# Four numerator tiles and six raw-row tiles in a linear attention followed by two feed-forward layers

## The chip, the cores and the metric

The kernel runs on one core of a Trainium2 chip. The metric is the time of one execution in microseconds (us) on the device, as the median of several runs. The engines are called TensorE (PE; its weight loads are PEld), VectorE (DVE), ScalarE (ACT), GpSimd (POOL) and SyncE (SP). Each runs its own instructions in the order in which they were written for it; an instruction that has to wait holds back all that stand behind it on its engine. GpSimd and SyncE issue most of the DMA transfers.

## What is computed

```
def _attn_ref(q, k, v, w_phi):            # q, k, v: 4 x 8 x 576 x 64
    def phi(x):
        proj = np.einsum('bhsd,df->bhsf', x, w_phi)              # f = 128
        proj = proj - np.max(np.abs(proj), axis=-1, keepdims=True)
        return np.concatenate([np.exp(proj), np.exp(-proj)], axis=-1)
    q_p, k_p = (phi(q), phi(k))
    kv = np.einsum('bhsf,bhsd->bhfd', k_p, v)
    z = np.sum(k_p, axis=2)
    num = np.einsum('bhsf,bhfd->bhsd', q_p, kv)
    den = np.einsum('bhsf,bhf->bhs', q_p, z)[..., None] + 1e-06
    return num / den

x = attention output as 2304 x 512
h = np.maximum(np.maximum(x @ w1, x @ w2), x @ w3)               # 768 wide
x = h @ w_out                                                    # 512 wide
h = x @ w_in                                                     # 2048 wide
g = np.maximum(h, 0.0) + alpha * np.minimum(h, 0.0)
out = g @ w_out2                                                 # 2304 x 512
```

## The kernel before

The kernel works through attention and the layers of the two feed-forward blocks. The attention goes pair by pair: four batches with four pairs of heads each, sixteen pairs in the loop at lines 467 to 489. For each pair, `keys` builds the features of the keys and multiplies them with the values (line 306, tile `kvp`); `queries`, which runs one pair behind, builds the features of the queries and the numerators: `num` (line 346) multiplies them into one PSUM bank `pn` at a time, and ScalarE copies each bank to a tile `nd` (line 357). One head's `nd` holds the numerators in one half of the partitions and the denominator in the rows of the other, so a pair takes two `nd` tiles.

After that GpSimd gathers the denominators by DMA into `dc` (line 388), moves the second head's numerators into the first tile (line 389), and, once VectorE has formed the reciprocals (lines 390 and 391), writes them out to `r_d` (line 393) and reads them back spread over the partitions into two raw tiles `xr` (line 400). `make_x` then multiplies `xr` with `nd` (line 414, GpSimd in the first pairs, VectorE in the others) and splits the result into a high part `x` (line 64, ScalarE) and a low part (line 70), the operands of layer 1. A tile `nd` is free again only after the product of line 414, a raw tile `xr` only after the split.

Layer 1 (`layer1`, line 436) takes groups of twelve matmuls of 288 columns, `p`, 48 units of three groups; a unit of a batch needs the `x` of all four pairs of that batch. The units of one batch are written between the pairs of the next, and those of the last batch behind the last pair (line 639). From the end of the last keys on, the weights of the later layers are staged: SyncE loads them into three tiles `st` (line 509), ScalarE and VectorE convert them (lines 77, 80, 84 and 86), and part of them goes out to `q_d` again (line 543). The staging tiles lie in the memory that the pool with the keys' tiles leaves. Then come layer 2 (`p`, line 691), layer 3 (`sums`, `pb`, `pc`, line 789) and layer 4 (`acc`, line 877).

The order of the instructions on each engine is written by a scheduler, which goes by priorities (the `high_priority` blocks), by what is ready in its own model and by which tiles are free: an instruction that needs a tile is placed only where one of that tag is free. So the number of buffers of a tag changes the order of all engines. `nd` lies in the pool `lp`, `xr` in the pool `xs_`; the pools that open after them take over that memory.

Of the kernel before, what the change touches and what calls it, by code (L numbers as in the profile page):

```python
# [9 lines left out]
F32 = mybir.dt.float32  # L10
# [11 lines left out]
P = 128  # L22
B, H, S, D = 4, 8, 576, 64
# [8 lines left out]
CH = S // 2  # L32
# [15 lines left out]
def tile_kernel(ctx: ExitStack, tc: tile.TileContext, qT, kT, tails, v, w_phi, w1, w2, w3, w_out, w_in, w_out2, alpha, out):  # L48
# [20 lines left out]
    def sub(eng, dst, src, hi):  # L69
        eng.tensor_tensor(dst, src, hi.bitcast(F32), op=ALU.subtract)  # L70
# [38 lines left out]
    def bank(tag, bufs, nm):  # L109
        return ps.tile([P, 512], F32, tag=tag, bufs=bufs, name=nm)  # L110
# [3 lines left out]
    xs_ = l1_ctx.enter_context(tc.tile_pool(name="xs", bufs=1, side="left"))  # L114
# [4 lines left out]
    def at(shape, dtype, name, tag=None, bufs=1):  # L119
        pool = ap if (tag or name) in KEYS_ONLY else lp  # L120
        return pool.tile(shape, dtype, name=name, tag=tag or name, bufs=bufs)
# [37 lines left out]
    def plain_kv(pair):  # L159
        return pair[0] < 2  # L160
# [57 lines left out]
    def project_queries(pair):  # L218
        ops = features(pair, "q")
        for g, tiles in enumerate(GROUPS):  # L220
            pp = at([P, 4, P], F32, tag="pp", bufs=2, name="pp")
            less_max(*project(ops, tiles), pp)
            yield g, tiles, pp
# [39 lines left out]
    def products(dst, ops, **kw):  # L263
        for i, (x, y) in enumerate(ops):
            nc.tensor.matmul(dst, x, y, start=i == 0, stop=i == len(ops) - 1, **kw)  # L265
# [69 lines left out]
    def queries(pair):  # L335

        parts = ("q",) if plain_kv(pair) else ("qh", "ql")
        qf = []
        for n, (o, w) in enumerate(CHUNKS):
            qf.append([])  # L340
            for x in parts:
                tag = f"qh{n}" if x != "ql" and pair[1] % 2 * len(x) != 1 else f"ql{n}"
                qf[n].append(at([P, 2, 2, w], F32 if plain_kv(pair) else F32R, tag=tag, bufs=1, name=x))
        nd = [at([P, S], F32, tag="nd", bufs=3, name="nd") for _ in range(2)]

        def num(n):
            o, w = CHUNKS[n]
            kv = kvs_of[pair]
            for h in range(2):
                pn = bank("p1", 3, "pn") if pair[0] == 0 else bank("pn", 1, "pn")  # L350
                ops = []
                for s in range(2):
                    q_ = [t[:, h, s] for t in qf[n]]
                    k_ = [t[:, h, s] for t in kv]
                    ops += [(k_[0], x) for x in q_] + [(x, q_[0]) for x in k_[1:]]
                products(pn[:, :w], ops)
                A.activation(nd[h][:, o : o + w], pn[:, :w], AF.Copy)  # L357

        def tail():
            yield 2, (0,), tail_of[pair]  # L360

        for g, tiles, pp in chain(project_queries(pair), tail()):
            o, w = (0, 2 * P, SM)[g], ST if g == 2 else 2 * P
            pt = bank("pn" if pair[0] == 0 and g == 1 else "pt", 1, "pt")
            for i in range(len(tiles)):
                for h in range(2):
                    c = h * len(tiles) * P + i * P
                    nc.tensor.transpose(pt[:, c : c + P], pp[:, 2 * i + h], ident)  # L368
            n = min(g, 1)
            dst = [t[:, :, :, o - CHUNKS[n][0] : o - CHUNKS[n][0] + w] for t in qf[n]]  # L370
            if plain_kv(pair):
                e = dst[0]
            else:
                e = at([P, 2, 2, 256], F32, tag="qe", bufs=2, name="qe")[:, :, :, :w]
            pv = pt[:, : 256 * len(tiles)].rearrange("p (h s) -> p h s", h=2)[:, :, -w:]
            A.activation(e[:, :, 0], pv, AF.Exp)
            A.activation(e[:, :, 1], pv, AF.Exp, scale=-1.0)
            if not plain_kv(pair):
                (hi_dve if g == 1 else hi_act)(dst[0], e)
                sub(V, dst[1], e, dst[0])  # L380
            yield
            if g != 1:
                num(n)
        yield
        dc = at([P, S // D], F32, tag="dc", bufs=2, name="dc")
        for h in range(2):
            dr = D * (1 - h)
            nc.gpsimd.dma_start(dc[h * D : (h + 1) * D], nd[h][dr : dr + 1].rearrange("a (p n) -> a p n", p=D))
        nc.gpsimd.dma_start(nd[0][D:], nd[1][D:])
        V.tensor_scalar(dc, dc, EPS, None, op0=ALU.add)  # L390
        V.reciprocal(dc, dc)
        rows = r_d[pair[0], pair[1]]
        nc.gpsimd.dma_start(rows.rearrange("h (p n) -> (h p) n", p=D), dc)
        raw = []
        for c in range(2):
            xr = raw_tile()
            for h in range(2):
                r = slice(h * D, (h + 1) * D)
                src = rows[h : h + 1, c * CH : (c + 1) * CH]
                nc.gpsimd.dma_start(xr[r], src.to_broadcast([D, CH]))  # L400
            raw.append(xr)
        waiting.append((pair, nd[0], raw))
        if pair[0] == 0 or pair[1] == NPAIR - 1:
            make_x(False)
# [3 lines left out]
    def make_x(pinned=True):  # L408

        pair, num_, raw = waiting.pop(0)  # L410
        res = []
        for c, xr in enumerate(raw):
            e = G if i_of(pair) < NPAIR - 1 else V
            x = e.tensor_tensor(xr, num_[:, c * CH : (c + 1) * CH], xr, op=ALU.mult)
            if pinned:
                tc.keep_in_program_order(x)
            xh, xl = x_tiles(c)
            if e is G:
                G.tensor_copy(xh, xr)
            else:  # L420
                hi_act(xh, xr)
            sub(e, xl, xr, xh)
            res.append((xh, xl))
        xs[pair[0]].append(res)

    def raw_tile():
        return xs_.tile([P, CH], F32, tag="xr", bufs=3, name="xr")

    def x_tiles(half):
        t = x_tile(half)  # L430
# [36 lines left out]
    for i, pair in enumerate(pairs):  # L467
        if i + 1 < len(pairs):
            load_pair(pairs[i + 1])
        with tc.high_priority(offset=(0, SOON, NOW, NOW)[pair[0]]):  # L470
            if i == PLAIN - 1:
                hi_dve(wph, wraw)
                sub(V, wpl, wraw, wph)
            run(*([at_priority(LATER, queries(last))] if last else []), keys(pair))
            last = pair
        count = CONVERT_IN[i] if i < len(CONVERT_IN) else 0
        for j in range(count):
            for _ in range(min(count, 4) if j == 0 else int(j + 3 < count)):
                fetch(begun[pair])
            with tc.high_priority(offset=LAST if i < NPAIR - 1 else 0):  # L480
                n = sum(len(x) for x in w)
                run(split_w123(n // 3, n % 3))
        u0 = 3 * (i - NPAIR) - LAG
        for u in range(u0, u0 + 3):
            if u >= 0:
                c, f = (u % 2, u // 2) if u < 12 else (u // NF1 % 2, u % NF1)
                layer1(u // 12, c, f, xs[u // 12], w[f])
        if waiting:
            make_x()
    ap_ctx.close()  # L490
    sp = ctx.enter_context(tc.tile_pool(reuse_waits="tile", name="sp", bufs=1, side="right"))
    with tc.high_priority(offset=NOW):
        run(queries(last))
# [128 lines left out]
    def load_h(c, kk):  # L622
        hi, lo = x_tile(c % 2), x_tile(c % 2)
        for k in range(2) if c == 0 else (slice(None),):
            if c == 0:
                hr = raw_tile()
                nc.sync.dma_start(hr, h_d[2 * kk + k, :, :CH])
            else:
                hr = early.pop(0) if c == 1 else fetch_h(c, kk)
            hi_act(hi[:, k], hr)  # L630
            sub(V, lo[:, k], hr, hi[:, k])
        for k in range(2):
            hs[c, 2 * kk + k] = (hi[:, k], lo[:, k])
# [29 lines left out]
    def double(tag, nm):  # L663
        t = ps.tile([P, 2, 512], F32, tag=tag, bufs=2 if tag == "da" else 1, name=nm)
        return t, t[:, :, :CH]
# [153 lines left out]
    for n, (tp, q) in enumerate(units):  # L819
# [4 lines left out]
        _, pb = double("db", "pb")  # L824
# [4 lines left out]
        _, pc = double("dc", "pc")  # L829
# [128 lines left out]
```

## Time and profile before

| | us |
|---|---|
| time, median of 3 runs | 883.45 (882.95 to 883.57) |
| the profiled execution | 883.95 |
| its span in the profile | 882.2 |
| TensorE busy in it | 868.6 (98%) |
| VectorE, ScalarE, GpSimd busy | 644.8, 506.8, 142.8 |

Busy time of TensorE is counted from pipelined matmuls whose ends are modelled, so neighbours overlap; how fast it works is read from the distance between starts. A time in a timeline or a chain is counted from the start of the span. The bracket behind a row says how long the engine was idle before it and what ended that. In the names `a<-b`, `a` is the tile written and `b` what is read.

### The profile page before, as it was taken

Reading aid. Unit: us, or ns where it says so; the run is one execution under the profiler, and the core shown is the slowest. Engines: PE = TensorE matmul, PEld = TensorE weight load, DVE = VectorE, ACT = ScalarE, POOL = GpSimd, SP = SyncE. Lnnn points to the kernel's source line nnn. Section 1 sums busy time; section 2 is a strip of 40 time slices with the busy share of each in tenths; the row PEclk is TensorE's granted clock in tenths of the full one; section 3 lists DMA queues with packets and bytes.
Section 4 is the critical chain, followed back from the end, with each engine's and each line's share of the span. In section 5 each row is a group of like instructions: output and inputs, shape, how many; then the busy total and the mean of one; then the engine's idle time right before and its main releaser. Section 6 shows DMA issues by size and latency. Waiting matters only on the chain.

```text
span 882.2 us, 17448 instructions
## 1 busy us (share of the span) xinstructions
PE 868.6 (98%) x6631; PEld 856.1 (97%) x6631; DVE 644.8 (73%) x1214; ACT 506.8 (57%) x1037; POOL 142.8 (16%) x250
## 2 busy tenths in 40 slices
PE   9999999999999999969999999999999999999998
PEld 8888999999999999969999999999999999999998
DVE  5578999778677767859964354746478999988781
ACT  4566676757764765666853354646477663544440
POOL 0354212213122222311101101111111000000000
PEclk9999999999999999989999999999999999999999
DMA  6445652313222149986556663655347756543321
GB/s 233 144 152 169 205 166 75 90 53 91 84 77 76 36 141 355 361 284 227 160 175 196 223 206 130 205 190 184 117 155 249 275 161 196 147 135 120 120 73 48
DMA packets 72227, 142.98 MB, mean 162 GB/s; under 512 B 9152, under 2 KB 36176, under 8 KB 72144
## 3 DMA queue, kind: packets, MB, share of 16 engines
q1 hardware_dynamic: 57696, 100.29, 35.9%
q0 software_dynamic: 12576, 37.92, 12.7%
q10 hardware_dynamic: 1872, 3.67, 1.3%
q8 instruction: 52, 0.85, 0.4%
q14 instruction: 31, 0.25, 0.1%
HBM read 93.07 MB, written 46.34 MB: 158 GB/s over the span
## 4 chain that ended last, share of the span: by engine, by line
PE 89%; DMA 5%; DVE 3%; ACT 1%; issue 1%; POOL 0%; ACTq 0%; DVEq 0%; POOLq 0%
PE p L265 22%; PE acc L877 20%; PE sums L789 12%; PE p L691 9%; PE pc L789 6%; PE pj L265 5%; PE pn L265 5%; PE kvp L306 3%; PE pb L789 3%; PE kvp L293 3%; DMA st<-in_w_out 2%; PE pt L368 2%; DMA st<-in_w_in 1%; DMA dc<-nd 1%; DMA nd<-nd 0%
## 5 line engine op out<-in xcount | busy, mean ns | idle before, releaser
L265 PE MATMUL p<-x,w123t 128*128 128x288 f32 x1728 | 253.2, 299 | 6.9 <-ACT x L64 6.9
L265 PEld LDWEIGHTS p<-x,w123t 128*128 128x128 f32 x1728 | 236.4, 190 | 8.2 <-ACT x L64 7.2
L789 PE MATMUL sums<-x,wi 128*128 128x288 f32 x768 | 107.6, 295 | 0.0
L877 PE MATMUL acc<-wq,o 128*128 128x256 f32 x864 | 105.5, 283 | 0.0
L877 PEld LDWEIGHTS acc<-wq,o 128*128 128x128 f32 x864 | 104.2, 189 | 0.0
L789 PEld LDWEIGHTS sums<-x,wi 128*128 128x128 f32 x768 | 103.9, 188 | 0.0
L877 PE MATMUL acc<-wq,x 128*128 128x256 f32 x648 | 78.1, 280 | 0.0
L877 PEld LDWEIGHTS acc<-wq,x 128*128 128x128 f32 x648 | 77.0, 188 | 0.0
L691 PE MATMUL p<-x,wo 128*128 128x288 f32 x576 | 76.6, 295 | 0.0
L691 PEld LDWEIGHTS p<-x,wo 128*128 128x128 f32 x576 | 76.5, 188 | 0.0
L808 DVE SCALAR_TENSOR_TENSOR g<-neg,al,g 128x576 f32<-128x576 f32 x64 | 50.3, 812 | 23.6 <-ACT neg L807 23.6
L212 DVE TENSOR_REDUCE mx<-pj 128x4 f32<-128x512 f32 (+1 forms) x80 | 50.3, 630 | 17.2 <-PE pj L265 17.0
L797 ACT ACTIVATE s<-sums 128x576 f32<-128x576 f32 x48 | 31.0, 647 | 42.0 <-PE sums L789 41.9
L455 POOL DMA_DIRECT2D h_d<-ho x48 | 28.9, 602 | 147.4 <-DVE ho L453 133.6
L809 POOL DMA_DIRECT2D g_d<-g x32 | 22.9, 715 | 166.1 <-DVE g L808 149.3
L357 ACT ACTIVATE nd<-pn 128x256 f32<-128x256 f32 (+1 forms) x64 | 26.4, 419 | 39.6 <-PE pn L265 25.2
L77 ACT ACTIVATE wt<-st 128x512 f16<-128x512 bf16 x38 | 30.1, 796 | 27.3 <-DMA st<-in_w_out 16.9
L293 PEld LDWEIGHTS kvp<-v,ke 128*128 128x128 f32 x320 | 40.9, 191 | 3.0 <-ACT ke L246 0.5
L807 ACT ACTIVATE neg<-g 128x576 f32<-128x576 f32 x64 | 40.1, 675 | 6.2 <-DVE g L839 5.9
L293 PE MATMUL kvp<-v,ke 128*128 128x128 f32 x320 | 42.6, 277 | 0.1
L64 ACT ACTIVATE o<-wt 128x512 fp32r<-128x512 f32 x45 | 27.4, 626 | 24.9 <-PE acc L877 15.1
L245 ACT ACTIVATE ke<-pj,mx 128x128 f32<-128x128 f32 x96 | 36.7, 382 | 7.5 <-DVE mx L212 7.5
(160 smaller groups left out, 1765.0 us busy)
## 6 DMA issues: line engine op xcount, KB each, us to landing
g_d<-g POOLq DMA_DIRECT2D x32, 576.0 KB, 3.6
a<-g_d SPq DMA_DIRECT2D x36, 512.0 KB, 4.6
st<-in_w_out SPq DMA_DIRECT2D x22, 512.0 KB, 6.1
wst<-in_w SPq DMA_DIRECT2D x18, 512.0 KB, 4.4
st<-in_w_in SPq DMA_DIRECT2D x16, 512.0 KB, 4.6
yr<-y_d SPq DMA_DIRECT2D x28, 288.0 KB, 3.5
v<-in_v SPq DMA_DIRECT2D x16, 480.0 KB, 4.2
q_d<-wt SPq DMA_DIRECT2D x28, 256.0 KB, 6.6
```

The lines of the kernel that those rows point to most:

```text
L77: order(A.activation(half[:, :, 1].bitcast(F16), lanes[:, :, 3].bitcast(BF16), AF.Copy))
L212: V.tensor_reduce(mx, pv, axis=AX.X, op=ALU.max, apply_absolute_value=True, negate=True)
L245: A.activation(ev[:, a, 0], pv[:, a], AF.Exp, bias=mx[:, a : a + 1])
L265: nc.tensor.matmul(dst, x, y, start=i == 0, stop=i == len(ops) - 1, **kw)
L293: nc.tensor.matmul(kvp[:, j * P : (j + 1) * P], e[:, c], rv[:, t, j // 2 : j // 2 + 2].rearrange("p a d -> p (a d)"), start=first, stop=t ...
L455: nc.gpsimd.dma_start(h_d[f, :, o : o + CH], ho)
L691: nc.tensor.matmul(p2[m // 2][1][:, m % 2], x, y, start=k + n == 0, stop=k == NF1 - 1 and n == 2)
L789: nc.tensor.matmul(dst[:, j], a, b, start=start and n == 0, stop=n == len(ops) - 1, skip_group_check=True)
L797: A.activation(s, src, AF.Copy)
L807: A.activation(neg, gv[:, j], AF.Relu, scale=-1.0)
L808: V.scalar_tensor_tensor(gv[:, j], neg, al[:, f + j : f + j + 1], gv[:, j], op0=ALU.mult, op1=ALU.add)
L877: nc.tensor.matmul(acc[i], x, y, start=half == 0 and f == 0 and n == 0 and place[i][1] == 0, stop=half == 1 and f == 3 and n == 2, skip_gr ...
```

## The change

The tag `nd` gets four buffers instead of three, and the tag `xr` six instead of three. No instruction is added or taken away; the scheduler writes another order. The two pools grow by 2304 and 3456 bytes in each partition.

```
--- before.py
+++ after.py
@@ -341,7 +341,7 @@
-        nd = [at([P, S], F32, tag="nd", bufs=3, name="nd") for _ in range(2)]
+        nd = [at([P, S], F32, tag="nd", bufs=4, name="nd") for _ in range(2)]
@@ -424,7 +424,7 @@
     def raw_tile():
-        return xs_.tile([P, CH], F32, tag="xr", bufs=3, name="xr")
+        return xs_.tile([P, CH], F32, tag="xr", bufs=6, name="xr")
```

In the rows of the order that follow, tiles carry the numbers in which the code makes them: `p1_` is a group of layer 1, `pn_4885`, `pn_4922` and `pn_4930` are numerators of the last pair, `nd_4850` and `nd_4851` its two tiles, `x_4952` its first `x`, and `st_` and `wt_` are weight loads and what they are converted to. TensorE around the last numerator of the last pair, before:

```order
L265 MATMUL p1_4789<-x_3588,w123t_1364 128x288 x3
L265 MATMUL p1_4802<-x_2621,w123t_1372 128x288 x3
L265 MATMUL p1_4802<-x_2992,w123t_1372 128x288
L265 MATMUL pn_4930<-qh_4848,kvh_4695 128x320
L265 MATMUL pn_4930<-ql_4849,kvh_4695 128x320
L265 MATMUL pn_4930<-qh_4848,kvl_4696 128x320
```

The same place after the change:

```order
L265 MATMUL p1_4407<-x_3359,w123t_1756 128x288 x3
L265 MATMUL p1_4407<-x_3584,w123t_1756 128x288 x3
L265 MATMUL pn_4930<-qh_4848,kvh_4695 128x320
L265 MATMUL pn_4930<-ql_4849,kvh_4695 128x320
L265 MATMUL pn_4930<-qh_4848,kvl_4696 128x320
```

The numerator has moved from the middle of group 4802 to the end of group 4407. TensorE where it first reads the last pair's `x`, before:

```order
L265 MATMUL p1_5180<-x_4835,w123t_787 128x288 x3
L265 MATMUL p1_5193<-x_4101,w123t_795 128x288 x3
L265 MATMUL p1_5193<-x_4472,w123t_795 128x288 x3
L265 MATMUL p1_5193<-x_4835,w123t_795 128x288 x3
L265 MATMUL p1_5104<-x_4952,w123t_318 128x288
L265 MATMUL p1_5117<-x_4952,w123t_465 128x288
```

And after:

```order
L265 MATMUL p1_5104<-x_4101,w123t_318 128x288 x3
L265 MATMUL p1_5104<-x_4472,w123t_318 128x288 x3
L265 MATMUL p1_5104<-x_4835,w123t_318 128x288 x3
L265 MATMUL p1_5117<-x_4101,w123t_465 128x288 x2
L265 MATMUL p1_5104<-x_4952,w123t_318 128x288
L265 MATMUL p1_5117<-x_4101,w123t_465 128x288
```

Before, six groups (5104 to 5193) had been begun with the `x` of the other three pairs before the first `x_4952` was read; now it is read in the second group. ScalarE at the copy of the last pair's numerator `pn_4885`, before:

```order
L357 ACTIVATE nd_4850<-pn_4877 128x256
L64 ACTIVATE x_4476<-xr_4322 128x288
L77 ACTIVATE wt_5357<-st_5286 128x512
L80 ACTIVATE st_5286<-st_5286 128x512
L77 ACTIVATE wt_5413<-st_5293 128x512
L357 ACTIVATE nd_4851<-pn_4885 128x256
```

And after:

```order
L77 ACTIVATE wt_5357<-st_5286 128x512
L80 ACTIVATE st_5286<-st_5286 128x512
L450 ACTIVATE s1_4375<-p1_4336 128x288
L64 ACTIVATE x_4101<-xr_3948 128x288
L77 ACTIVATE wt_5413<-st_5293 128x512
L80 ACTIVATE st_5293<-st_5293 128x512
L357 ACTIVATE nd_4851<-pn_4885 128x256
```

In both the copy stands at the 13th weight load (`st_5293`), now behind both steps of it; the copy of the numerator before it (`nd_4850<-pn_4877`), which stood two loads ahead, now stands six loads ahead.

## Rows read from the trace of the kernel before

**Rows 1.** The page, busy us (share of the span) and instructions of an engine.

```profile
PE 868.6 (98%) x6631; PEld 856.1 (97%) x6631; DVE 644.8 (73%) x1214; ACT 506.8 (57%) x1037; POOL 142.8 (16%) x250
```

**Rows 2.** TensorE's waits: who waited for whom, us in total, times, longest.

```profile
PE p L265 <- ACT x L64: 6.9, 1, 6.9
PE warm L130 <- DVE signs L132: 1.1, 1, 1.1
PE pj L265 <- DVE pp L216: 0.8, 1, 0.8
PE pn L265 <- ACT q L376: 0.4, 1, 0.4
```

**Rows 3.** Timeline of TensorE: start, us, line, out<-in, xcount, idle before.

```profile
319.53 0.28 PE L306 MATMUL kvp<-kl,vh 128*128 128x256 f32 x1
...
362.21 0.31 PE L265 MATMUL pn<-qh,kvh 128*128 128x320 f32 x1
...
367.01 0.31 PE L265 MATMUL pn<-qh,kvl 128*128 128x320 f32 x1
367.16 17.91 PE L265 MATMUL p<-x,w123t 128*128 128x288 f32 x134
392.00 0.61 PE L265 MATMUL p<-x,w123t 128*128 128x288 f32 x1 [6.93 <-ACT x L64]
```

**Rows 4.** The chain that ended last: start, us, what; layer 2.

```profile
443.85 76.45 PE p L691 x576
```

**Rows 5.** Stretches: length, busy us of the engines, granted clock, DMA share, GB/s.

```profile
375.00:380.00 5.00, 5.00 (x40) 5.00 (x39) 3.02 (x10) 2.04 (x6) 0.62 (x2) 1.00 1.04 391
...
388.00:389.00 1.00, 0.00 (x0) 0.00 (x0) 0.00 (x0) 0.00 (x0) 0.00 (x0) 0.87 1.06 330
391.00:392.00 1.00, 0.00 (x1) 0.00 (x1) 0.35 (x1) 1.00 (x3) 0.00 (x0) 0.50 0.38 152
...
395.00:396.00 1.00, 1.00 (x8) 1.00 (x7) 1.00 (x3) 1.00 (x3) 0.00 (x0) 0.72 1.10 389
```

**Rows 6.** The chain that ended last, 300 to 400.

```profile
384.72 5.35 DMA st<-in_w_in
...
390.16 0.09 DVE wt L84
...
390.52 0.45 DVE xr L414
...
391.52 0.44 ACT x L64
...
392.00 8.07 PE p L265 x47
```

**Rows 7.** Timeline of GpSimd, last pair.

```profile
368.34 0.53 POOL L388 DMA_DIRECT2D dc<-nd x1 [0.39 <-ACT nd L357]
...
383.59 2.11 POOL L400 DMA_DIRECT2D xr<-r_d x4 [2.37 <-DMA r_d<-dc]
```

**Rows 8.** Timeline of ScalarE, 355 to 370.

```profile
356.61 0.38 ACT L357 ACTIVATE nd<-pn 128x256 f32<-128x256 f32 x1 [0.87 <-DVE xr L414]
...
359.52 0.68 ACT L80 ACTIVATE st<-st 128x512 uint32<-128x512 uint16 x1
360.09 0.40 ACT L450 ACTIVATE s<-p 128x288 f32<-128x288 f32 x1
```

**Rows 9.** What SyncE's queue waited for, 300 to 330.

```profile
SPq L509 <- DVE kl L70: 47.3, 1, 47.3
...
SPq L509 <- PE kvp L306: 2.9, 1, 2.9
```

**Rows 10.** The tile `st`, 300 to 400: from issue to landing.

```profile
DMA to landing us min/median/max: 3.6/5.7/8.6
```

**Rows 11.** GpSimd's waits in the whole span.

```profile
POOL xr L400 <- DVE x L70: 12.6, 7, 3.2
```

## Prediction

> **What bounds the kernel now.** I read the busy times of the page first. TensorE is busy for 98% of the span and its weight loads for 97% [rows 1], so time can be won only where TensorE stands still or runs slowly. The next view is therefore TensorE's own waits [rows 2]: there is one large one, 6.9 us, in which a layer-1 product waits for ScalarE to write an `x`; the next are 1.1 us at the start of the kernel, 0.8 and 0.4 us. The timeline places the large one [rows 3]: a run of 134 layer-1 matmuls that starts at 367.16 is followed by one at 392.00.
>
> What is it worth? Matmuls of this shape are issued 76.45 / 576 = 0.1327 us apart where nothing holds them up [rows 4], so without the wait the next would have started at 367.16 + 134 x 0.1327 = 384.94: 7.06 us lost. Then the granted clock [rows 5]: it falls to half, the 1.2 GHz level, in the microsecond from 388 (mean 0.87), is 0.50 when the matmuls begin again, and returns to 2.4 GHz in the one from 395 (0.72). By the chain, 47 matmuls took 8.07 us from 392.00 [rows 6], against 47 x 0.1327 = 6.24: another 1.83 us. **The stall costs 8.9 us in all**, 1% of the time.
>
> As a check on the second term: the Trainium skill, "TensorE: Matmul & The Clock Gate", Terms, puts the penalty at the throttled time times the share of clock taken away. By that, an estimate, 6.8 us at half clock would cost 3.4 us, and the forecast below would be 1.6 us lower. The rows disagree, since only 3.6 of those 6.8 us fall behind 392.00; I go by the rows.
>
> What ended last? Two legs meet there. One is the last pair's: its last numerator (`pn`) ends on TensorE at 367.16 [rows 3], GpSimd starts the denominators' DMA at 368.34 and fetches the raw rows from 383.59 on [rows 7]. The other is the weights', and by the chain [rows 6] it ended last: the conversion of the weight load issued at 384.72 (5.35 us) stands on VectorE, at 390.16, ahead of the product `xr` at 390.52, and ScalarE's copy to `x` follows at 391.52. From the end of the last numerator to the first matmul that reads this `x` it is 392.00 - 367.16 = **24.8 us, of which TensorE had work for 134 matmuls, 17.8 us**. The difference is the wait.
>
> **The change, part by part.** No instruction is added or removed. More buffers let the scheduler write another order, and the order is what counts.
>
> *Numerator tiles.* A pair takes two. With three, the next pair's must wait until one is free: ScalarE stood 0.87 us at 356.61 for VectorE's `xr` to let go of one [rows 8]. Such waits are small, but the order was built around them: it held numerators back behind layer-1 products. Counted in the order, 1216 matmuls of 288 columns stand ahead of the end of the last pair's last numerator before, and 1101 after; the counts of all other matmuls ahead of it are equal. So it ends 115 x 0.1327 = 15.3 us earlier, at about 351.9. Between it and the first matmul that reads the last pair's `x` stood 134 matmuls and stand now 206: **27.3 us of cover instead of 17.8, for a chain that took 24.8**. The margin is 2.5 us, and the wait of 7.06 us with its half-speed stretch of 1.83 goes.
>
> *The weights' leg must come forward as well.* It is tied to the last pair: the queue of SyncE stood 47.3 us until VectorE had split that pair's keys, then 2.9 us for their products on TensorE, before it could issue weight loads [rows 9], because the staging tiles take over the keys' memory. The last of these products, at 319.53 [rows 3], has 127 fewer matmuls of 288 columns ahead of it, and 10 more of 256, so it moves forward by some 15.7 us, and the 23rd load from 390 to about 374.4. Both legs shift alike. The first matmul on the last `x` stands 43 places sooner, at 384.94 - 43 x 0.1327 = 379.2; the legs arrive at 376.3 to 376.7. That is the same margin from the other side.
>
> *Is the 24.8 us still the chain's length?* In the new order VectorE's `xr` and ScalarE's `x` stand behind row groups of layer 1 which TensorE finishes 21.1 and 22.7 us after the last numerator (159 and 171 matmuls). With ScalarE's copies (0.40 [rows 8] and 0.44 [rows 6]), its step on the weights (0.68 [rows 8]) and some issue, `x` can't be ready before about 24.3. So 24.3 is the lower end, 24.8 my value because the same work stands in it. The upper end comes from the weight loads: from issue to landing they took 3.6 to 8.6 us, against 5.35 for the one on the chain [rows 10]; 3.3 us more gives 28.1, that is 0.8 us beyond the cover.
>
> *Raw-row tiles.* GpSimd waited 12.6 us in seven pieces for VectorE to release a raw tile before it could fetch the next rows [rows 11]. These waits go, at nothing for the time: none of TensorE's waits is for them, because layer-1 work of an earlier batch covers the products. Where that cover is gone, it is the chain above. The loads of `h` for layer 2 use the same tag and can start sooner; TensorE has no wait there now, so it is worth nothing.
>
> *Memory.* Two pools grow by 5760 bytes per partition, and later pools lie elsewhere. No TensorE wait of over 0.4 us is listed for a line of layer 1's end or of what follows it [rows 2], and the order of its matmuls is the same again from some 100 matmuls after the stall. I take zero, and up to 1 us if a later tile now waits for an older one.
>
> *Small new waits.* From the fifth pair up to 370 the order on TensorE, VectorE and ScalarE is rewritten; its small waits there were 0.8 and 0.4 us. The new ones lie between none (a gain of 1.2) and twice as many (a loss of 1.2). I put down 0.5 us of loss, since the margins of the new order are thinner at two places.
>
> **Sum.** The profiled run took 883.95 us, with a span of 882.2: 883.95 - 7.06 - 1.83 + 0.5 = 875.6. The median is 0.5 us below that run, so 875.0 for the median.
>
> **The rivals.**
>
> *Part of the wait stays.* For it: both legs depend on DMA that is full, with a share of 1.04 in 375 to 380 [rows 5], and the margin is 2.5 us. Each microsecond of lateness beyond it is lost, and a long wait costs clock too, as it did here, where it fell in the fourth microsecond. A wait of 2 to 5 us with up to 1.8 of clock gives 877.1 to 881.9. Against it: the DMAs of the two legs are the same as before, and both legs move by the same 15 us.
>
> *No change.* TensorE waits as long for the last `x`, because the chain behind the last numerator has grown from 24.8 to 27.3 + 7.1 = 34.4 us: 883.4, 881.7 to 885.2. Against it: the same DMAs and copies stand in the chain. The Trainium skill, "Perfetto Trace Analysis", Optimization Strategy, speaks for this one: it takes a gap that repeats on the saturated engine as the sign of too few buffers. Here the gap comes once, so by that rule buffers are not its cause and the time stays. The rows bear out that the gap is single; they also show ScalarE waiting for a numerator tile, which is why this gets a small chance.
>
> *Slower: numerators queue behind weight loads.* In the new order ScalarE's copy of the last pair's second numerator stands behind the conversion of the 13th weight load (shown above with the change), and TensorE's next numerator needs the bank that this copy empties. Before, that next numerator stood at 362.21 [rows 3], now it stands at 346.9. The 13th conversion ended at 359.52 + 0.68 = 360.2 and the copy takes 0.38 [rows 8]: 360.6, or 344.9 if the loads come forward by 15.7. Margin 2.0 us. If the loads are late by d against that, TensorE waits d - 2.0 there. It is slower by more than 0.2% once that wait passes 8.9 us, which is d above 10.9: the loads come forward by less than 4.8 us. If they don't move at all the wait is 13.7, with 1.8 for the clock 15.5 instead of 8.9, so 890.0. The last `x` then has its cover and adds nothing. Against it: the SyncE rows tie the loads to the keys, which do move.
>
> **How the numbers follow.** A difference of under 0.2%, 1.8 us, can hardly be told from none here. Forecast, 874 to 877: 0.61. Part of the wait stays, 877 to 881.7: 0.17. No change: 0.12. Slower, 885.2 to 890: 0.10. The likeliest gives 875.0. The low end is 883.45 - 8.9 with 0.8 us for a small wait that goes: 873.8. To hold 8 in 10 the range takes in the rival with part of the wait and the beginning of the next: 882.2. Faster by over 0.2%: 0.61 + 0.17 = 0.78; within: 0.12; slower: 0.10.
>
> **What would show it.** Right: in the profile after, the list of TensorE's waits holds nothing above some 2 us, the granted clock stays 1.00 around 380, the last numerator ends near 352, SyncE's weight loads begin some 15 us earlier, and all that follows the stall is some 8.5 us earlier. Wrong: a wait of several microseconds for `x` near 379 (the chain grew), or one for ScalarE's `nd` near 347 (loads late), or several new waits of a microsecond between 60 and 300 (the new order is too tight for the engines behind it).

## The result and the profile after

The change makes the kernel faster: 876.42 us median (876.16 to 877.49, six runs) against 883.20 for the kernel before beside it, a ratio of 0.9918 with an interval of 0.9903 to 0.9932. The medians differ by 6.8 us and the ratio stands for 7.2; the median is 1.4 us above the 875.0 forecast. In the profiles the span falls from 882.2 to 874.9 us.

The large wait is gone. TensorE's waits after the change, with the columns of [rows 2]:

```profile
PE warm L130 <- DVE signs L132: 1.1, 1, 1.1
PE kvp L293 <- ACT ke L245: 0.9, 1, 0.9
PE p L265 <- ACT s L450: 0.5, 1, 0.5
PE pj L265 <- DVE pp L216: 0.4, 1, 0.4
PE kvp L293 <- ACT ke L246: 0.3, 1, 0.3
```

Nothing for an `x` is left, and the longest wait but for the first is 0.9 us. In their place stand three waits that the kernel before did not have, for `ke` (twice) and for `s`, 1.7 us together.

The timeline of TensorE at the last numerator answers to [rows 3]:

```profile
353.28 0.31 PE L265 MATMUL pn<-qh,kvl 128*128 128x320 f32 x1
353.42 46.87 PE L265 MATMUL p<-x,w123t 128*128 128x288 f32 x353
```

The run of layer-1 matmuls that followed the last numerator started at 367.16 and stopped after 134; it now starts at 353.42 and goes on without a pause. The stretches show the same with the clock, columns as in [rows 5]:

```profile
350.00:400.00 50.00, 50.00 (x380) 50.00 (x378) 40.88 (x89) 33.17 (x60) 9.72 (x18) 1.00 0.87 284
375.00:380.00 5.00, 5.00 (x40) 5.00 (x39) 4.32 (x12) 3.66 (x10) 0.63 (x2) 1.00 0.92 292
380.00:385.00 5.00, 5.00 (x40) 5.00 (x39) 5.00 (x12) 4.66 (x10) 0.54 (x1) 1.00 0.97 290
```

TensorE is busy for all of the 50 us in which it had stood for 6.9, at the 2.4 GHz level throughout. DMA is about as full as before, a share of 0.87 to 0.97.

The two legs to the last pair's `x`, first the weights' (SyncE's first issue, ScalarE's and VectorE's first steps on the 23rd load, the latter at 390.16 in [rows 6]), then ScalarE's writing of `x`, which stood at 391.52:

```profile
303.10 11.29 SPq L509 DMA_DIRECT2D st<-in_w_out  x5
...
376.39 0.81 ACT L77 ACTIVATE wt<-st 128x512 f16<-128x512 bf16 x1 [1.34 <-DMA st<-in_w_in]
...
376.56 0.46 DVE L84 TENSOR_SCALAR wt<-st 128x512 uint16<-128x512 uint16 x1
...
377.90 1.10 ACT L64 ACTIVATE x<-xr 128x288 fp32r<-128x288 f32 x3
```

The first of the three `x` in the last row is the one in question, written at about 378.3. TensorE reads it 206 matmuls after 353.42, at 353.42 + 206 x 0.1327 = 380.8. So the chain took 378.3 - 353.42 = 24.9 us, the cover is 27.3, and 2.4 us are to spare. The same start of SyncE's loads stood here before:

```profile
316.57 12.10 SPq L509 DMA_DIRECT2D st<-in_w_out  x5
```

It is 13.5 us later, and 390.16 is 13.6 us later than 376.56: the two legs moved together. The weights' leg came last again: the raw rows had landed at 375.9 by the trace, and ScalarE still waited for the load, which landed at 376.4.

A landmark that is easy to read in every profile is the start of layer 2 in the chain of waits, since all that follows takes the same time (882.2 - 443.85 = 438.4 us before, 874.9 - 436.52 = 438.4 after). Before it was 443.85 [rows 4]; after the change:

```profile
436.52 13.52 PE p L691 x102
```

So the whole difference, 7.3 us, lies ahead of layer 2. To divide it I take the start of a matmul less the sum of the distances at which all matmuls ahead of it are issued when nothing holds them up (0.1327 us for 288 columns, and so for the other shapes). From 345 us to layer 2 this loss grows by 9.0 us before and by nothing after (-0.2): the 8.9 us of the forecast. Between 48 and 150 us it grows by 2.7 us before and by 4.6 after: 1.9 us are lost again, far from the stall. 9.2 - 1.9 = 7.3. Some 0.3 of these 1.9 lie ahead of 49 us, where no new order can be the reason: TensorE's own differs only from 65 us on, ScalarE's from 49.

### The profile page after: what moved, and what is told of

The parts are those of the page before. It is cut to its first block, busy times and chain, and to the rows that moved or that the text cites. A ratio compares the mean times of both kernels' runs of the same rounds, so it can differ in the third digit from the quotient of the medians.

```text
span 874.9 us, 17414 instructions
## 1 busy us (share of the span) xinstructions
PE 867.9 (99%) x6631; PEld 855.1 (98%) x6631; DVE 643.0 (73%) x1214; ACT 507.8 (58%) x1037; POOL 141.2 (16%) x250
## 4 chain that ended last, share of the span: by engine, by line
PE 97%; DVE 2%; DMA 1%; issue 1%; ACT 0%; POOL 0%; DVEq 0%; ACTq 0%
PE p L265 26%; PE acc L877 21%; PE sums L789 12%; PE p L691 9%; PE pj L265 6%; PE pc L789 6%; PE pn L265 6%; PE kvp L293 3%; PE kvp L306 3%; PE pb L789 3%; PE pt L368 2%; PE kvt L325 0%; PE warm L130 0%; DMA xr<-r_d 0%; DMA r_d<-dc 0%
## 5 line engine op out<-in xcount | busy, mean ns | idle before, releaser
L265 PE MATMUL p<-x,w123t 128*128 128x288 f32 x1728 | 249.3, 298 | 0.5 <-ACT s L450 0.5
L455 POOL DMA_DIRECT2D h_d<-ho x48 | 27.3, 568 | 161.1 <-DVE ho L453 129.6
L246 ACT ACTIVATE ke<-pj,my 128x128 f32<-128x128 f32 x96 | 37.5, 390 | 2.8 <-DVE my L243 2.7
```

The lines of the kernel that those rows point to most:

```text
L246: A.activation(ev[:, a, 1], pv[:, a], AF.Exp, bias=my[:, a : a + 1], scale=-1.0)
```

## The experiments

Three theories at first. A: the order decides. `x` is late by the chain behind the last numerator less the matmuls that TensorE has meanwhile. B: the number of tiles as such, those for raw rows among them, frees the engines. C: it is the place of later tiles in memory.

**Raw rows alone** (raw_alone).

```
-        return xs_.tile([P, CH], F32, tag="xr", bufs=3, name="xr")
+        return xs_.tile([P, CH], F32, tag="xr", bufs=6, name="xr")
```

> Six tiles for raw rows, three for numerators as before. Theory A (the order behind the last numerator decides): in the written order 131 layer-1 matmuls stand between the last numerator and the first one on the last pair's x, 17.4 us for a chain of 24.8, so a wait for that x of 2.6 us or more stays; 881 to 884 us if the numerator's leg ends last, about 878 if the weights' leg does, which is one weight load shorter here. Rival B (the raw tiles decide, since GpSimd waited 12.6 us for them before): no wait at that x, about 876 us.

Ratio 1.0005 (0.9994 to 1.0015): no gain. Its TensorE waits and the place in its timeline:

```profile
PE p L265 <- ACT x L64: 7.4, 1, 7.4
...
368.06 17.55 PE L265 MATMUL p<-x,w123t 128*128 128x288 f32 x131
393.00 27.27 PE L265 MATMUL p<-x,w123t 128*128 128x288 f32 x191 [7.39 <-ACT x L64]
```

GpSimd's 12.6 us of waiting for raw tiles [rows 11] no longer appear, and nothing comes of it. `x` is there 24.9 us after 368.06, for a cover of 131 x 0.1327 = 17.4. Rival B falls for the raw rows.

**Numerators alone** (num_alone).

```
-        nd = [at([P, S], F32, tag="nd", bufs=3, name="nd") for _ in range(2)]
+        nd = [at([P, S], F32, tag="nd", bufs=4, name="nd") for _ in range(2)]
```

> Four tiles for numerators, three for raw rows as before. Theory A (the order behind the last numerator decides): 222 matmuls, 29.5 us, of cover for a chain of 24.8; no wait at the last pair's x, and the same early small waits as with the full change (1.9 us more than before): 875 to 877 us. Rival B (the raw tiles decide): GpSimd's waits for raw tiles stay and so does TensorE's wait of some 7 us: about 883 us.

Ratio 0.9911 (0.9895 to 0.9928): the whole gain of the change. No wait for `x`, and the three small waits of the full change:

```profile
PE kvp L293 <- ACT ke L245: 0.9, 1, 0.9
PE pj L265 <- DVE pp L216: 0.7, 1, 0.7
PE p L265 <- ACT s L450: 0.5, 1, 0.5
PE kvp L293 <- ACT ke L246: 0.3, 1, 0.3
```

**More memory, nothing else** (pad_same_order, pad_new_order).

```
-        dc = at([P, S // D], F32, tag="dc", bufs=2, name="dc")
+        dc = at([P, S // D + 900], F32, tag="dc", bufs=2, name="dc")[:, : S // D]
```

> The tile for the gathered denominators is given 900 more columns that nothing uses; two buffers, so 7200 bytes per partition more, as a bound above the 5760 of the change. The order of instructions is that of the kernel before on every engine. Theory A (order decides): the wait of 6.9 us stays, 883.2 us, within 1 us. Rival C (where the later tiles lie in memory decides): about 876 us, as with the change.

Ratio 0.9993 (0.9982 to 1.0004), a wait of 5.6 us at the same place. The second kernel has 720 in place of 900:

> The same tile with 720 more columns that nothing uses, 5760 bytes per partition as in the change; three numerator and three raw tiles. With that room the scheduler writes another order from the thirteenth pair on: 238 matmuls, 31.6 us, of cover behind the last numerator, the order before it as in the kernel before, the last keys no sooner. Theory A (the order behind the last numerator decides, not the count of tiles): no wait at the last pair's x and none of the new small waits of the fifth pair: 883.2 - 8.9 = 874.3 us. Rival B (tile counts as such decide): 883 us. Rival D (the weights' leg has to come forward too, by way of the last keys): a wait at that x stays, 877 to 882 us.

This expectation was wrong on the kernel itself: its order is that of the kernel before on every engine, 134 matmuls behind the last numerator, so that it is a second run of the first kind, with exactly the bytes of the change. Ratio 0.9995 (0.9983 to 1.0006), a wait of 6.4 us. Together they show that moving the later tiles by as much memory is worth nothing (theory C falls; the padding lies in one pool, the change's bytes in two), and how far the stall differs between runs of one order: 5.6, 6.4 and 6.9 us.

**Own tiles for the last pairs.** The next kernels give the last pairs a tag of their own, so that the order changes at the end alone, and by different amounts. With 14 and four buffers it reads:

```
-        nd = [at([P, S], F32, tag="nd", bufs=3, name="nd") for _ in range(2)]
+        nd = [at([P, S], F32, tag="nd" if i_of(pair) < 14 else "nd2",
+                 bufs=3 if i_of(pair) < 14 else 4, name="nd") for _ in range(2)]
```

> Only the last two pairs take their numerator tiles from a tag of their own, with four buffers; the other pairs keep three, raw rows three. On TensorE the order is that of the kernel before up to the last pairs, so the small waits of the fifth and sixth pairs are those of before, and the last keys end no sooner. 248 layer-1 matmuls, 32.9 us, stand behind the last numerator; 18 weight loads instead of 23 stand ahead of the last pair's x. Theory A (wait = chain of 24.8 us behind the last numerator less the cover): no wait at x, 883.2 - 8.9 = 874.3 us, that is 2 us below the full change. Rival E (the weight loads have to begin sooner, which here they don't): a wait of some microseconds at x, 877 to 883 us.

Ratio 0.9898 (0.9878 to 0.9918), no wait for `x`: as theory A says for the stall. The weight loads began no sooner than before, and `x` was written at 380.46, ahead of its place at 350.91 + 248 x 0.1327 = 383.8:

```profile
317.61 4.04 SPq L509 DMA_DIRECT2D st<-in_w_out  x3
...
350.91 85.61 PE L265 MATMUL p<-x,w123t 128*128 128x288 f32 x645
...
380.01 0.45 ACT L64 ACTIVATE x<-xr 128x288 fp32r<-128x288 f32 x1 [1.34 <-DVE xr L414]
```

So rival E falls in the form given: the loads need not begin sooner where fewer of them (18, not 23) stand ahead of `x`. But the span, 874.9, is that of the full change, not 2 us less. From 345 us to layer 2 some 0.9 us are lost, and 3.6 between 48 and 150, where the profile of before lost 2.7. Most of the 0.9 is a new wait, which is the slower rival of the prediction in miniature: ScalarE waits for a weight load, its copy of a numerator stands behind the load's two steps, and TensorE's next numerator waits for the copy.

```profile
343.71 0.80 ACT L77 ACTIVATE wt<-st 128x512 f16<-128x512 bf16 x1 [2.94 <-DMA st<-in_w_out]
...
345.44 0.36 ACT L357 ACTIVATE nd<-pn 128x256 f32<-128x256 f32 x1
...
345.86 0.41 PE L265 MATMUL pn<-qh,kvh 128*128 128x320 f32 x1 [0.63 <-ACT nd L357]
```

The same edit with 15, so that the last pair alone has its own tiles:

> The same with the last pair alone on four tiles of its own. 164 layer-1 matmuls, 21.8 us, stand behind the last numerator, and 22 weight loads ahead of the last pair's x. Theory A: a wait at x of 24.8 - 21.8 = 3.0 us, with no loss of clock since that fell in the fourth microsecond of the wait before: 883.2 - 8.9 + 3.0 = 877.3 us (876.5 to 878.5). Rival (a threshold: tiles are enough or not): 874.3 or 883.2 us.

Ratio 0.9991 (0.9975 to 1.0008): no gain, and the expectation missed. The wait was 5.0 us, not 3.0, and a second of 0.8 followed. From 345 us to layer 2 the loss was 8.2 us, some 0.9 less than before; between 48 and 150 us this profile lost 4.4 us, 1.7 more than that of before, which hid it there:

```profile
364.58 21.89 PE L265 MATMUL p<-x,w123t 128*128 128x288 f32 x164
391.47 4.46 PE L265 MATMUL p<-x,w123t 128*128 128x288 f32 x18 [5.01 <-ACT x L64]
396.76 3.48 PE L265 MATMUL p<-x,w123t 128*128 128x288 f32 x24 [0.83 <-ACT s L450]
```

The cover was as counted, 21.8 us; the chain took 26.8 instead of 24.8. Two engines show why, VectorE and then GpSimd:

```profile
383.02 0.69 DVE L86 TENSOR_TENSOR wt<-wt,st 128x512 uint32<-128x512 uint32 x1 [1.07 <-ACT st L80]
383.63 0.45 DVE L453 TENSOR_TENSOR ho<-p,s 128x288 f32<-128x288 f32 x1
...
384.38 0.54 POOL L455 DMA_DIRECT2D h_d<-ho  x1 [7.93 <-DVE ho L453]
384.91 2.21 POOL L400 DMA_DIRECT2D xr<-r_d  x4
```

GpSimd could not fetch the last pair's raw rows (line 400) because an issue of layer 1's result (`h_d`) stood ahead of them and waited 7.9 us for VectorE. TensorE had finished that group 110 matmuls after 364.58, at 379.2; VectorE came to it at 383.63, because a step on a weight load stood ahead, which waited for ScalarE's step on the same load. **The weights' leg thus reaches `x` by way of GpSimd's queue**, and it ended last here: the numerators had come forward, the loads had not. The clock fell too, in the third microsecond of the wait (388 to 389, mean 0.84):

```profile
388.00:389.00 1.00, 0.00 (x0) 0.00 (x0) 0.46 (x1) 0.78 (x1) 0.00 (x0) 0.84 0.88 270
```

The same edit with 10:

> The last six pairs on four tiles of their own, seven numerator tiles in all, more than in the change. The written order gets worse: the last pair's four numerators stand in one row, 64 layer-1 matmuls, 8.5 us, behind them, and ScalarE's copies of the second to fourth stand behind the conversion of 24 weight loads. Theory A with the order read as it stands: TensorE waits some 17 us for such a copy at about 374 us (the 24th load was converted at 391.6 before), then 24.8 - 8.5 = 16.3 us at x: 883.2 - 8.9 + 33 + 2 for the clock = about 909 us (900 to 912). Rival B (more tiles, fewer waits): 874 to 877 us.

Here again the expectation had the order wrong: the kernel that ran has 224 matmuls (29.7 us) behind the last numerator, not 64, and nothing in it starves the numerators. Ratio 0.9916 (0.9893 to 0.9939) and no wait for `x`, which for 224 matmuls is what theory A gives. The slow case that it was to show was not tried.

The same edit with 8:

> The last eight pairs on four tiles of their own. The order is that of the kernel before up to the eighth pair; 242 layer-1 matmuls, 32.1 us, stand behind the last numerator, and the last keys end 78 places sooner. Theory A: no wait at x; and if the 1.9 us that the full change lost against the sum are the new small waits of the fifth and sixth pairs, they are not there: 874.3 us (873.5 to 875.3). Rival F (the 1.9 us belong to the longer cover or to the later tiles): 876.2 to 877 us.

Ratio 0.9895 (0.9876 to 0.9914), no wait for `x`, but the span is 874.8, as with the full change. Theory A holds; that the 1.9 us would not be there did not come out in this profile. Its loss between 48 and 150 us was 4.0 us, though its order up to 160 us is that of the kernel before, in which the loss was 2.7. So the loss differs between runs of one order, and one pair of profiles can't tell what the new order costs there. The last four runs, side by side, were for that, and for a case that must be slower:

> The changed kernel once more, beside the three that follow. Theory G: the loss between 50 and 106 us differs from run to run of one and the same order (2.7 to 4.4 us so far in eight profiles with the order of the kernel before in that stretch), and the new order there adds about 1.3 us to the mean: the loss is 4 to 5.5 us in this profile too, and the ratio to the kernel before is 0.990 to 0.993. Rival H: the new order adds nothing there, the two high values (4.6 and 5.0) were chance: 3.5 us and a ratio equal to that of the two kernels with the old order there.

> The last eight pairs on four tiles of their own once more. Up to the eighth pair its order is that of the kernel before. Theory G: about 1 us faster than the full change in the same call (ratio lower by 0.001 to 0.002). Rival H: as fast as the full change, within 0.5 us.

> The last two pairs on four tiles of their own once more. Theory G: about 1 us faster than the full change in the same call, less 0.6 for the wait for ScalarE's copy that it showed at 345.9. Rival H: 0.5 us slower than the full change. Theory A in either case: no wait at the last pair's x.

The ratios to the kernel before were 0.9919 (0.9902 to 0.9935) for the full change, 0.9907 (0.9892 to 0.9923) with 8 and 0.9915 (0.9899 to 0.9930) with 14; the medians 877.02, 875.77 and 876.61 us. The loss between 48 and 150 us in all profiles:

| order in that stretch | profiles | us lost between 48 and 150 |
|---|---|---|
| as before | 11 | 2.7, 2.7, 2.9, 3.1, 3.2, 3.4, 3.6, 3.9, 4.0, 4.1, 4.4; mean 3.5 |
| as in the change | 3 (after, num_alone, full_again) | 4.6, 4.9, 5.0; mean 4.8 |

By this count the two groups don't overlap, but that hangs on where it starts: in three profiles (after, raw_alone, own_two_again) 0.4 to 0.5 us of the loss lie between 48 and 50 us (0.0 to 0.2 in the others), ahead of any difference in TensorE's order. Counted from 50 us on, own_last_one, which has the order of before there, lost as much (4.2 us) as the profile of after (4.2). A count without issue distances puts them as close: all kernels have the same matmuls among their first 300 (up to 50.6 us in the profile of before) and among their first 700 (up to 109.9). From the one place to the other it took longer than in the profile of before by 1.6, 2.2 and 2.3 us in the new order, and by -0.1 to 1.5, mean 0.7, in the old one. So theory G holds for the means: the new order costs about 1.4 us there, and a single pair of profiles can't show it. The waits in the timeline show half of it: those of that stretch come to 2.1 to 2.4 us in the three profiles (among them the three for `ke` and `s`, which no other has there) and to 1.1 to 1.9, mean 1.5, in the eleven. The other half is no idle time by the profile: all idle time of TensorE there comes to hardly more than the listed waits. It lies in longer distances between starts, some of it at the waits themselves, as the stall of before, listed with 6.93 us, took 7.1 by starts. The profile of before was at the low end of its own spread, which is why the pair of profiles shows 1.9. What makes a run of one order lose 2.7 us or 4.4 there was not found.

The last kernel has 12 and three buffers, six numerator tiles in all, but never more than three for one pair's neighbours:

> The last four pairs take their numerator tiles from a tag of their own with three buffers: six numerator tiles in all, but never more than three for these pairs. 115 layer-1 matmuls, 15.3 us, stand behind the last numerator, fewer than before (134); its end by the order is at 369.7. Theory A: x is ready at 369.7 + 24.8 = 394.5, its place in the order is at 384.9, a wait of 9.6 us with some 2 us of clock: 883.2 - 8.9 + 9.6 + 2 = 885.9 us (884.5 to 888), slower than before. Rival B (the count of tiles as such decides): 874 to 877 us.

Ratio 1.0032 (1.0018 to 1.0046): slower, as forecast. The wait is where it was expected, at 9.8 us for 9.6:

```profile
370.81 15.41 PE L265 MATMUL p<-x,w123t 128*128 128x288 f32 x115
396.01 24.19 PE L265 MATMUL p<-x,w123t 128*128 128x288 f32 x170 [9.79 <-ACT x L64]
```

Rival B is done with: six tiles lose time, seven win it or not, four win it; it is the order that follows from them. All stages of that comparison in one table (chain: from the start of the run behind the last numerator to the end of ScalarE's writing of `x`):

| kernel | matmuls of cover, us | chain, us | chain less cover | TensorE's wait for `x` |
|---|---|---|---|---|
| own_four_of_three | 115, 15.3 | 25.2 | 9.9 | 9.8 |
| raw_alone | 131, 17.4 | 24.9 | 7.5 | 7.4 |
| before | 134, 17.8 | 24.8 | 7.0 | 6.9 |
| pad_new_order | 134, 17.8 | 24.2 | 6.4 | 6.4 |
| pad_same_order | 134, 17.8 | 23.5 | 5.7 | 5.6 |
| own_last_one | 164, 21.8 | 26.8 | 5.0 | 5.0 |
| after | 206, 27.3 | 24.9 | -2.4 | none |
| num_alone | 222, 29.5 | 26.3 | -3.2 | none |
| own_last_six | 224, 29.7 | 26.3 | -3.4 | none |
| own_last_eight | 242, 32.1 | 29.5 | -2.6 | none |
| own_last_two | 248, 32.9 | 29.5 | -3.4 | none |

The wait is chain less cover in every row. That is arithmetic, since both are read from one trace; what was staked ahead of the runs, where the order was read rightly, is the wait: 9.6 us in own_four_of_three (9.8 measured), 6.9 in pad_same_order (5.6), 2.6 or more in raw_alone (7.4), 3.0 in own_last_one (5.0), and none in num_alone, own_last_two and own_last_eight (none). The chain is no constant: where there is room, `x` stands behind more of layer 1 on VectorE and ScalarE, and where the weights press, it waits for them.

A version that beats both kernels is the one with 8 and four buffers, if any: 875.77 against 877.02 us side by side, some 1.2 us, about what the mean of the table above would give (1.4). The intervals of the two ratios overlap, so this is likely, not shown.

## Why the prediction was right, and where it was off

*The stall's worth, 8.9 us: right.* From 345 us to layer 2 the loss fell from 9.0 us to nothing. By starts the stall took 7.1 us of it and the slow matmuls behind it 1.7; the rest, 0.2 to 0.4, lay ahead of it, most at 346.30, where a numerator waited 0.3 us for a copy behind a weight load. The forecast left this rest out and took the clock's part 0.2 too high: 1.83 counts to the end of the 47th matmul (400.07), not to the start of the next (399.91). In the other kernels with a stall, the matmuls behind the wait took 1.4 to 2.6 us more than their distances. The estimate from the Trainium skill ("TensorE: Matmul & The Clock Gate", Terms: throttled time times the share of clock taken away) again comes out too high: with a wait of 9.8 us the half clock lasted from about 388.7 to 399.0, 5 us by that rule, and 1.5 were lost.

*Numerators 115 matmuls sooner: right.* The last one was forecast to end at 351.9 and ended at 353.4. The 1.5 us are for the most part the loss in the fifth and sixth pairs, which shifted everything behind it.

*Cover 27.3 us for a chain of 24.8, margin 2.5: right,* with 24.9 and 2.4 measured. The reason given, that the same work stands in it, held for this order; in others the same work took 23.5 to 29.5 us.

*The weights' leg "must come forward as well": half right.* It came forward by 13.5 us (15.7 less the early loss) and arrived with the other. own_last_one shows a leg that doesn't come forward and then sets the end. own_last_two shows that it need not, where `x` is placed ahead of more loads. What counts is how many loads stand ahead of `x` and of the issues ahead of it in GpSimd's queue, a route that the prediction did not name.

*Raw-row tiles and memory at zero: right,* by raw_alone (1.0005) and the two padded kernels (0.9993, 0.9995). Half of the change does nothing.

*Small new waits, 0.5 us within -1.2 and 1.2: mis-sized.* It was 1.9 us in the pair of profiles and 1.4 on the mean, beyond the bound. The bound was the step that failed: it doubled the 1.2 us of waits that the list of before shows between 60 and 300, but that stretch lost 2.7 us in the same profile, and up to 4.4 in others. The list holds idle time alone; the loss against the matmuls' own distances also holds the longer distances between starts in which the profile shows none. With 1.9 in place of 0.5 the sum is 883.95 - 8.9 + 1.9 - 0.5 = 876.5, and 876.4 was measured. That this fits so closely is in part luck, since the 1.9 are one pair of profiles and runs of one order differ by 1.7 us there.

*The rivals.* "No change" is what raw rows alone give. The step from a gap that comes once to a cause other than buffers did not hold: this one went with one more buffer of one tag (num_alone, 0.9911). "Part of the wait stays" is own_last_one. "Numerators queue behind weight loads" showed itself at 0.6 us in own_last_two and at 0.3 in the kernel before (346.30), not in the change, where ScalarE's copy was done 2.2 us ahead of need (346.2 for 348.46; 2.0 forecast).

## What to carry to other kernels

Where a scheduler writes the order, read a buffer count as an edit to the order: count, at the wait that costs the time, the work that now stands between its cause and its place, and set it against the chain's length. Follow that chain through every queue that it passes, since a slow stranger ahead of one issue (here a weight load, by way of VectorE and GpSimd) lengthens it as surely as its own work. And size small losses by start times against the sum of issue distances, in more than one profile, not by a list of waits.

## What the runs showed of the hardware

Runs of one and the same order lose 2.7 to 4.4 us on TensorE between 48 and 150 us, and the stall for `x` differs by 1.3 us between them (5.6 to 6.9), while everything behind the start of layer 2 takes 438.4 us in both kernels. The price of the half clock did not grow with the wait: by starts of the matmuls behind it, it was 2.0, 1.4, 2.6, 1.7, 1.8 and 1.5 us for waits of 5.0, 5.6, 6.4, 6.9, 7.4 and 9.8 us. Nor did the clock fall at a fixed time after the matmuls stopped: 3.8 us after (384.94 to about 388.7) in the kernel before, 2.3 us after (386.3 to about 388.7) in own_last_one.
